# A new decode of the first two weight matrices, and a new order of the first units, in an attention and two-layer MLP kernel

## The chip, the cores and the metric

The kernel runs on one core of one Trainium2 chip. The metric is the device time in microseconds (us). Before the change, three runs took 758.19, 758.59 and 758.95 us, with a median of 758.59 us.

## The reference

Every array arrives on the chip in its stored type. The attention inputs are 32-bit floats. The four weight matrices are 64-bit floats, and the chip has to make 32-bit values of them itself. This is called decoding below. The reference, cut to what matters:

```
state = 0                                          # per batch (4) and head (8): 48 x 48
for t in range(768):                               # gated linear attention
    y[t] = r[t] @ (state + (u * k[t]) outer v[t])
    state = w[t][:, None] * state + k[t] outer v[t]
x = y as (3072 tokens, 384)
h = x @ w_in                                       # 384 -> 1024
solu = h * softmax(h)
ln = (solu - mean) / sqrt(var + 1e-6) * g_ln
x = ln @ w_out                                     # 1024 -> 384
out = max(0.01 * h2, h2) @ w2_out, h2 = x @ w2_in  # 384 -> 2048 -> 384
```

## The kernel before

The 3072 tokens are cut into 24 units of 128 tokens. Six time blocks times four batches give unit i. A unit is prepared by VectorE scans and multiplies (`prep1` to `prep4`, `prep_k`, `prep_diag`), runs its attention on TensorE (`att_kt`, `att_scores`, `att_u`, `att_y`), is evacuated by VectorE (`att_x`), turned by TensorE (`x_t`), split into a high and a low part (`x_hi`, `x_lo`) and multiplied with the first weights (`mm1 i half`, nine matmuls of 512 columns for each half). The soft steps and `z_t`, `z_hi`, `z_lo` follow. `mm2a` and `mm2b` multiply three units together with the second weights (12 matmuls of 384 columns each). After all units, `mm3` and `mm4` run the second MLP for groups of 512 tokens.

Every product is made of three passes, high by high, high by low and low by high, so each weight is kept as a high tile (`w1ih`, `w1oh`) and a low tile (`w1il`, `w1ol`).

The schedule is written out by hand. `FIRST` is the text for units 0 to 9, `LOOP` for units 10 to 13 and `LAST` for the rest. Each name in it emits its instructions in that place, so the text sets the order on every engine's queue and on the DMA queue that SyncE issues. An engine runs its own queue in order.

The first weights are decoded inside `FIRST`, in 14 slices. Six slices are of `w_in`, 512 columns each, and eight of `w_out`, 384 columns each. Each slice is a tile `q` of pairs of 32-bit words (lower, upper) that a DMA has brought. Before the change a slice takes these steps.

- `w1_a` (L762): VectorE shifts the exponent out of the upper words (L199), and ScalarE turns it into a power of two (L201, with a bias read per partition).
- `w1_e` (L205, VectorE): the sign is put in.
- `w1_f` (L210, VectorE): the upper 20 mantissa bits are masked out in place.
- `w1_h` (L216, VectorE): the lower words, as floats times 2^-32, are added to them.
- `w1_b` (L221, VectorE): the sum is multiplied with the power of two, and for `w_out` also with `gl` (the factor g_ln).
- `w1_c`: ScalarE rounds the value to the high tile (L803). TensorE puts the value (L805, identity, recorded as two instructions) and minus the high tile (L806) together in the PSUM tile `PO`.
- `w1_d`: ScalarE copies `PO` to the low tile (L812).

`general` (L246) is a slow path for inputs out of range. It stands behind a branch at the end that the given inputs do not take. `mm1 4 0` is called the mark below. It is the first half of unit 4's product with the first weights, the first `mm1` behind all 14 slices.

Of the kernel before, what the change touches and what calls it, by code (L numbers as in the profile page):

```python
# [43 lines left out]
prep_state 1; w1_b; x_t 0; prep1 2; att_scores 1; att_mul_next 1; load_tr 3; x_hi 0; x_lm 0; w1_f; prep_k 2;  # L44
prep_diag 1; x_lo 0; att_evac_s 1; w1_d; prep_check 2; mm1 0 0; w1_c; w1_a; att_state 1; load_o 1; prep2 2; prep3 2;
prep_vd 1; att_kt 2; load_nat 2; w1_d; prep_state 2; w1_a; mm1 0 1; att_evac_k 2; prep1 3; prep_check 3; att_y 1;
att_u 2; prep4 2; soft_max 0; att_x 1; w1_e; load_tr 4; prep_k 3; soft_e 0; x_t 1; att_mid 2; att_scores 2; soft_z
0; w1_f; att_evac_s 2; w1_g; w1_h; prep_bonus 2; x_hi 1; x_lm 1; x_lo 1; mm1 1 0; w1_h; soft_nm 0; prep_check 4; mm1
1 1; soft_c 0; w1_e; w1_b; att_mul_next 2; z_t 0; prep2 3; w1_a; w1_f; w1_c; z_hi 0 0; att_kt 3; prep3 3; z_hi 0 1;
w1_a; w1_d; w1_e; w1_b; w1_h; z_lm 0 0; z_lm 0 1; w1_f; w1_c; w1_b; prep_state 3; z_lo 0 0; prep1 4; z_lo 0 1;  # L50
prep_state 4; prep4 3; w1_d; prep_diag 2; att_scores 3; att_y 2; w1_e; soft_max 1; prep_vd 2; soft_q 0; prep_k 4;
att_x 2; att_state 2; att_evac_k 3; w1_c; x_t 2; load_nat 3; soft_e 1; load_tr 5; x_hi 2; att_u 3; w1_d; att_mid 3;
x_lm 2; x_lo 2; soft_z 1; mm1 2 0; prep_bonus 3; att_evac_s 3; prep2 4; att_kt 4; soft_nm 1; w1_a; w1_f; w1_h;
soft_c 1; w1_e; w1_b; w1_h; w1_c; z_t 1; att_mul_next 3; load_nat 4; w1_a; w1_f; prep3 4; w1_d; mm1 2 1; soft_q 1;
z_hi 1 0; w1_h; w1_b; prep1 5; prep4 4; z_lm 1 0; att_state 3; prep_k 5; prep_diag 3; z_hi 1 1; w1_c; z_lm 1 1;
att_evac_k 4; prep_vd 3; z_lo 1 0; soft_max 2; att_u 4; att_mid 4; att_mul_next 4; z_lo 1 1; att_y 3; w1_d;
att_scores 4; w1_b; att_x 3; soft_e 2; w1_c; x_t 3; att_kt 5; soft_z 2; x_hi 3; prep_bonus 4; att_state 4; w1_e;
# [5 lines left out]
5; prep_k 6; z_t 3; z_hi 3 0; load_tr 7; att_kt 6; att_evac_s 5; z_lm 3 0; z_hi 3 1; mm1 4 1; mm2_out 4; z_lm 3 1;
prep1 7; prep_bonus 6; prep_k 7; mm2a 5; att_scores 6; soft_max 4; prep_state 6; prep_check 6; z_lo 3 0; z_lo 3 1;
prep_vd 5; load_nat 7; prep2 7; prep3 7; att_state 5; att_evac_k 6; load_tr 8; att_y 5; soft_q 3; att_u 6; prep_diag
6; soft_e 4; prep_bonus 7; att_x 5; soft_z 4; prep4 7; att_mid 6; soft_nm 4; att_kt 7; x_t 5; mm2b 5; prep_vd 6;
att_mul_next 6; prep_check 7; x_hi 5; x_lo 5; mm1 5 0; att_evac_s 6; prep1 8; soft_c 4; soft_q 4; z_t 4; load_nat 8;
prep_diag 7; mm1 5 1; z_hi 4 0; prep_vd 7; prep_k 8; z_hi 4 1; att_evac_k 7; z_lo 4 0; prep2 8; att_state 6; z_lo 4
1; load_tr 9; att_y 6; att_u 7; mm2_out 5; soft_max 5; att_x 6; prep_state 7; att_scores 7; att_kt 8; soft_e 5; x_t
6; prep_bonus 8; mm2a 6; att_mid 7; prep3 8; soft_z 5; att_mul_next 7; soft_nm 5; x_hi 6; mm2b 6; prep_state 8;  # L70
att_evac_k 8; x_lo 6; load_nat 9; mm1 6 0; prep_check 8; prep1 9; prep2 9; soft_c 5; soft_q 5; z_t 5; z_hi 5 0;
prep4 8; prep_bonus 9; att_evac_s 7; z_hi 5 1; z_lo 5 0; load_tr 10; mm1 6 1; mm2_out 6; att_state 7; z_lo 5 1;
prep_k 9; soft_max 6; att_u 8; att_y 7; att_scores 8; prep3 9; soft_e 6; att_x 7; mm2a 7; prep4 9; prep_check 9;
prep_diag 8; prep_diag 9; x_t 7; soft_z 6; load_nat 10; att_mid 8; mm2b 7; x_hi 7; x_lo 7; soft_nm 6; soft_c 6; mm1
7 0; att_mul_next 8; att_evac_s 8; z_t 6; prep_vd 8; z_hi 6 0; prep_state 9; att_kt 9; load_tr 11; att_state 8;
prep1 10; z_lo 6 0; z_hi 6 1; prep_k 10; z_lo 6 1; mm1 7 1; soft_max 7; att_y 8; prep_state 10; att_scores 9; soft_q
6; mm2_out 7; att_evac_k 9; prep2 10; att_x 8; prep_vd 9; att_u 9; soft_e 7; att_mid 9; att_kt 10; x_t 8; x_hi 8;
att_mul_next 9; mm2a 8; soft_z 7; att_evac_k 10; att_state 9; x_lo 8; soft_nm 7; soft_c 7; prep3 10; prep_check 10;
prep1 11; att_evac_s 9; mm1 8 0; z_t 7; mm1 8 1; z_hi 7 0; z_lo 7 0; z_hi 7 1; z_lo 7 1; soft_q 7; prep_bonus 10;
att_y 9; att_u 10; prep2 11; prep_check 11; prep_k 11; prep4 10; att_scores 10; prep3 11; prep_state 11; soft_max 8;  # L80
att_x 9; load_nat 11; mm2b 8; load_tr 12; prep_diag 10; x_t 9; soft_e 8; soft_z 8; att_mid 10; mm2_out 8; att_evac_s
10; att_kt 11; att_mul_next 10; soft_nm 8; mm2a 9; x_hi 9; prep4 11; x_lo 9; prep1 12; soft_c 8; soft_q 8; mm1 9 0;
# [1029 lines left out]
```

## Time and profile before

| what | value |
|---|---|
| median of three runs | 758.59 us |
| the profiled execution | 758.94 us |
| its span, first to last instruction | 757.2 us |
| around the span | 1.74 us |
| TensorE busy | 725.6 us (96%) |
| VectorE busy | 505.7 us (67%) |
| ScalarE busy | 359.9 us (48%) |

The spans of the engines overlap. In the rows, PE is TensorE's matmul, PEld its weight load, DVE VectorE, ACT ScalarE, POOL GpSimd and SPq the DMA queue. The time around the span is not seen by the profile. The rows of consecutive matmuls overlap (a row of 0.39 us, and the next one starts 0.23 us after it), so their spacing is read from their starts or from a run of many.

### The profile page before, as it was taken

What the parts mean: (1) busy time and instruction counts of PE and PEld (TensorE: products, weight loads), DVE (VectorE), ACT (ScalarE), POOL (GpSimd) and SP (SyncE); (2) the same over time, 40 slices, a digit from 0 to 9 for tenths busy, and PEclk for the clock granted to TensorE, in tenths of its full rate; (3) what the DMA queues carried; (4) which work ended last, traced back from release to release, by engine and by line L of the source; (5) the groups of instructions that cost most, each with busy time, mean ns of one, the idle gap of its engine ahead of it and who ended that gap; (6) DMA issues with size and microseconds to landing.
All of it is one profiled execution on the core that took longest, in us unless ns stands there. A gap on an engine that the chain in (4) does not pass through costs nothing.

```text
span 757.2 us, 15011 instructions
## 1 busy us (share of the span) xinstructions
PE 725.6 (96%) x6209; PEld 612.1 (81%) x6209; DVE 505.7 (67%) x851; ACT 359.9 (48%) x660; POOL 164.2 (22%) x184
## 2 busy tenths in 40 slices
PE   2799999999999999998999999999999999999996
PEld 1466889898989898997888888888888888888885
DVE  7799979878878888877899975453343334334332
ACT  4487675656565554665645543323232332332231
POOL 2335554455553434312000100001000100100000
PEclk9999999999999999999999999999999999999999
DMA  9723263344354343224363220050020001001001
GB/s 333 272 76 132 91 186 120 108 132 159 99 171 138 120 146 116 65 84 140 102 218 106 84 62 1 1 166 1 1 84 1 1 0 42 1 0 42 1 0 45
DMA packets 30606, 69.07 MB, mean 91 GB/s; under 512 B 3244, under 2 KB 15684, under 8 KB 30404
## 3 DMA queue, kind: packets, MB, share of 16 engines
q1 hardware_dynamic: 30532, 68.06, 27.0%
q8 instruction: 50, 0.82, 0.4%
q14 instruction: 24, 0.20, 0.1%
HBM read 58.59 MB, written 9.45 MB: 90 GB/s over the span
## 4 chain that ended last, share of the span: by engine, by line
PE 88%; DVE 8%; ACT 2%; issue 1%; DMA 1%; POOL 0%; SPq 0%; DVEq 0%
PE PK L915 13%; PE PZ L915 13%; PE PH L665 11%; PE PO L721 10%; PE PH L944 9%; PE PA L944 9%; PE PO L944 4%; PE PZ L944 4%; PE PZ L632 3%; PE PZ L613 3%; PE PA L721 2%; PE PZ L622 1%; PE PA L550 1%; PE PO L805 1%; PE PA L570 1%
## 5 line engine op out<-in xcount | busy, mean ns | idle before, releaser
L935 DVE TENSOR_TENSOR gw<-t,gh 128x512 fp32r<-128x512 f32 x96 | 68.4, 714 | 52.5 <-ACT gh L931 52.3
L931 ACT CAST gh<-t 128x512 fp32r<-128x512 f32 x96 | 59.6, 621 | 67.0 <-DVE t L927 51.5
L927 DVE TENSOR_TENSOR t<-t,PZ 128x512 f32<-128x512 f32 x48 | 32.9, 686 | 69.3 <-ACT t L923 69.2
L901 POOL TENSOR_TENSOR x2l<-x2l,x2h 128x1536 fp32r<-128x1536 f32 x4 | 14.1, 3531 | 287.5 <-ACT x2h L897 287.5
L927 DVE TENSOR_TENSOR t<-t,PK 128x512 f32<-128x512 f32 x48 | 33.0, 687 | 59.4 <-ACT t L923 59.2
L923 ACT ACTIVATE t<-PZ 128x512 f32<-128x512 f32 x48 | 28.7, 598 | 84.1 <-PE PZ L915 79.3
L923 ACT ACTIVATE t<-PK 128x512 f32<-128x512 f32 x48 | 28.7, 598 | 80.4 <-PE PK L915 75.0
L721 PE MATMUL PO<-zh,w1oh 128*128 128x384 f32 x168 | 59.8, 356 | 0.0
L665 PE MATMUL PH<-w1ih,xh 128*128 128x512 f32 x144 | 58.0, 403 | 0.8 <-DVE zbuf L677 0.8
L665 PE MATMUL PH<-w1ih,xl 128*128 128x512 f32 x144 | 56.8, 395 | 0.2
L665 PE MATMUL PH<-w1il,xh 128*128 128x512 f32 x144 | 56.5, 392 | 0.0
L721 PE MATMUL PO<-zh,w1ol 128*128 128x384 f32 x168 | 56.3, 335 | 0.0
L721 PE MATMUL PO<-zl,w1oh 128*128 128x384 f32 x168 | 56.3, 335 | 0.0
L915 PE MATMUL PK<-x2h,w2ih 128*128 128x512 f32 x144 | 56.2, 390 | 0.0
L915 PE MATMUL PK<-x2l,w2ih 128*128 128x512 f32 x144 | 56.1, 389 | 0.0
L915 PE MATMUL PZ<-x2h,w2il 128*128 128x512 f32 x144 | 56.1, 389 | 0.0
L915 PE MATMUL PZ<-x2l,w2ih 128*128 128x512 f32 x144 | 56.1, 389 | 0.0
L915 PE MATMUL PK<-x2h,w2il 128*128 128x512 f32 x144 | 56.0, 389 | 0.0
L915 PE MATMUL PZ<-x2h,w2ih 128*128 128x512 f32 x144 | 56.0, 389 | 0.0
L673 ACT ACTIVATE ebuf<-PH,nmax 128x1024 f32<-128x1024 f32 x24 | 26.8, 1116 | 39.3 <-DVE nmax L670 39.3
L670 DVE TENSOR_REDUCE nmax<-PH 128x1 f32<-128x1024 f32 x24 | 29.2, 1218 | 15.6 <-PE PH L665 15.5
L944 PE MATMUL PH<-gw,w2oh 128*128 128x512 f32 x96 | 37.4, 389 | 0.0
(189 smaller groups left out, 1955.6 us busy)
## 6 DMA issues: line engine op xcount, KB each, us to landing
tr<-in_trw_dram SPq DMA_DIRECT2D x23, 776.0 KB, 5.0
natq<-in_nat_q_dram SPq DMA_DIRECT2D x24, 384.0 KB, 4.6
w2s<-in_moe_w_in_dram SPq DMA_DIRECT2D x48, 128.0 KB, 2.6
w2s<-in_moe_w_out_dram SPq DMA_DIRECT2D x16, 384.0 KB, 3.2
natv<-in_nat_v_dram SPq DMA_DIRECT2D x24, 192.0 KB, 4.4
o_dram<-o SPq DMA_DIRECT2D x24, 192.0 KB, 1.9
x2l<-o_dram SPq DMA_DIRECT2D x6, 768.0 KB, 6.0
out_dram<-ot SPq DMA_DIRECT2D x18, 256.0 KB, 2.1
```

What stands on the lines that cost most here:

```text
L613: pe.matmul(out=y[64 * c:64 * c + 64, hs], lhsT=s[64 * c:64 * c + 64, x, q], rhs=a[64 * c:64 * c + 64, h], start=(h == 0), stop=False, ski ...
L632: pe.matmul(out=out, lhsT=x, rhs=ident, is_transpose=True, start=(n == 0), stop=(n == of - 1), skip_group_check=True)
L665: pe.matmul(out=PH[:, half], lhsT=a[:, kc], rhs=c[:, kc, 512 * half:512 * half + 512], start=(n == 0), stop=(n == 8))
L670: dve.tensor_reduce(out=nmax[:, i:i + 1], in_=flat(PH), axis=AX.X, op=ALU.max, negate=True)
L673: act.activation(out=ebuf, in_=flat(PH), func=AF.Exp, bias=nmax[:, i:i + 1], accum_out=s_all[:, i:i + 1])
L721: pe.matmul(out=o2[m], lhsT=a[:, c, 128 * m:128 * m + 128], rhs=d[:, c], start=(c == 0 and q == 0), stop=(c == K1 - 1 and q == 2))
L915: pe.matmul(out=h_at[n % 2], lhsT=a[:, kc, 128 * o:128 * o + 128], rhs=d[:, kc], start=(q == 0), stop=(q == 8))
L923: act.activation(out=gs[n][0], in_=h_at[n % 2], func=AF.Copy, scale=0.01)
L927: dve.tensor_tensor(out=t, in0=t, in1=h_at[n % 2], op=ALU.max)
L931: act.copy(out=gh, in_=t)
L935: dve.tensor_tensor(out=gw, in0=t, in1=f(gh), op=ALU.subtract)
L944: pe.matmul(out=at, lhsT=a[:, c % 4, 128 * o:128 * o + 128], rhs=d, start=(c == 0 and q == 0), stop=(c == K2 - 1 and q == 2))
```

## The change

The decode of the 14 slices is made of other steps, the sizes staying as they are. ScalarE reads the upper words as 32-bit floats and multiplies them by 2^-112 (`w1_a`). VectorE shifts the bits left by three (`w1_e`) and puts the sign in (`w1_f`), which gives the value without the lower words, in `t`. VectorE masks `t` to its signed power of two (`w1_h`), and multiplies that with the lower words and -2^-52 (for `w_out` also with g_ln) into the low tile itself (`w1_b`). In `w1_c` ScalarE multiplies a slice of `w_out` by g_ln, then rounds to the high tile, and TensorE adds a third product, minus the low tile, between the two others. `w1_d` is unchanged and overwrites the low tile.

The names in `FIRST` are the same 546 items in another order. `general` is rewritten with inner loops in place of unrolled code and with its decoded weights in DRAM. An unused pad of 96 columns becomes `gl2`, which holds g_ln times -2^-52. `LOOP` and `LAST` are unchanged.

```diff
 FIRST = """
-w1_a; prep1 0; load_w 1; prep_state 0; w1_e; prep2 0; load_w 2; load_w 3; load_tr 1; w1_f; prep3 0; prep_k 0; w1_h;
-load_nat 0; att_kt 0; prep_check 0; prep4 0; w1_a; w1_a; w1_b; w1_e; w1_e; w1_f; w1_c; w1_d; att_evac_k 0; load_o 0;
-w1_f; w1_h; w1_h; w1_a; w1_a; w1_b; w1_e; w1_c; w1_b; w1_e; att_u 0; load_g; load_u; w1_a; prep1 1; w1_f; load_nat
-1; w1_e; prep2 1; w1_h; prep_k 1; prep_check 1; prep3 1; w1_a; prep_bonus 0; w1_d; w1_f; att_scores 0; w1_b; att_kt
-1; prep4 1; w1_h; w1_f; w1_c; att_evac_k 1; att_mid 0; att_mul_next 0; prep_diag 0; w1_h; prep_vd 0; att_evac_s 0;
-att_state 0; w1_d; w1_b; w1_c; att_y 0; att_u 1; prep_bonus 1; load_tr 2; w1_d; att_mid 1; att_x 0; w1_e; w1_c;
...
-4; att_scores 5; prep_state 5; prep2 6; soft_q 2; att_mid 5; prep_bonus 5; soft_e 3; prep_check 5; mm2a 4; soft_z 3;
-soft_nm 3; x_t 4; x_hi 4; mm2b 4; att_mul_next 5; soft_c 3; prep3 6; load_nat 6; x_lo 4; mm1 4 0; prep4 6; prep_diag
...
+load_w 1; w1_a; prep1 0; w1_a; load_w 2; w1_e; w1_a; prep_k 0; w1_f; att_kt 0; prep2 0; w1_h; prep3 0; att_evac_k 0;
+load_w 3; w1_b; prep4 0; w1_e; w1_c; w1_a; load_tr 1; w1_e; w1_f; w1_f; w1_h; prep_check 0; w1_e; w1_d; w1_h; w1_f;
+w1_b; load_nat 0; w1_b; w1_a; w1_h; w1_c; w1_e; w1_b; w1_a; w1_d; w1_f; prep1 1; w1_c; w1_e; att_u 0; w1_h; prep_k
+1; load_u; w1_d; att_scores 0; load_tr 2; prep2 1; w1_c; prep_bonus 0; w1_d; att_kt 1; att_evac_k 1; w1_f; att_mid
+0; prep3 1; att_mul_next 0; prep_diag 0; prep_vd 0; prep_check 1; w1_b; att_evac_s 0; prep_check 2; load_nat 1;
+prep_state 0; att_y 0; att_state 0; w1_h; att_x 0; att_u 1; prep4 1; load_o 0; att_mid 1; prep1 2; w1_c; x_t 0;
+prep_state 1; w1_b; load_g; prep_bonus 1; w1_d; load_nat 2; load_tr 3; prep2 2; x_hi 0; att_mul_next 1; att_scores
+1; prep_diag 1; w1_c; w1_a; att_state 1; x_lm 0; x_lo 0; mm1 0 0; prep_k 2; att_evac_s 1; att_kt 2; w1_a; prep_vd 1;
...
+4; soft_e 3; prep_k 6; att_u 5; prep_check 5; load_nat 6; att_scores 5; prep2 6; att_kt 6; att_x 4; prep_bonus 5;
+soft_z 3; prep_state 6; x_t 4; att_mid 5; x_hi 4; x_lo 4; soft_nm 3; soft_c 3; att_evac_s 5; prep3 6; prep_check 6;
+load_tr 7; att_mul_next 5; prep_bonus 6; mm2a 4; mm1 4 0; prep_diag 5; z_t 3; mm1 4 1; z_hi 3 0; att_evac_k 6; z_lm
+3 0; prep4 6; z_hi 3 1; z_lm 3 1; prep1 7; mm2b 4; load_tr 8; att_scores 6; prep_vd 5; prep2 7; soft_max 4; soft_q
...
-        const.tile([128, 96], F32, name="pad")
+        gl2 = const.tile([128, 96], F32, name="gl2")[:, 0:K1]
...
-            decode_exp(nc, q, t, ebias)
+            act.activation(out=f(t), in_=f(q[:, :, 1]), func=AF.Copy, scale=2.0 ** -112)
...
+            top = q[:, :, 1]
             if n == 0:
-                decode_sign(nc, q, t)
+                dve.tensor_scalar(out=t, in0=t, scalar1=3, scalar2=None, op0=ALU.logical_shift_left)
             elif n == 1:
-                decode_top(nc, q)
+                dve.scalar_tensor_tensor(out=t, in0=top, scalar=-2147483648, in1=t, op0=ALU.bitwise_and,
+                                         op1=ALU.bitwise_or)
             elif n == 2:
-                decode_sum(nc, q)
+                dve.tensor_scalar(out=top, in0=t, scalar1=-8388608, scalar2=None, op0=ALU.bitwise_and)
             else:
-                x = f(q[:, :, 0])
-                decode_mul(nc, q, t, x, 2.0 ** -20 if key[0] == "i" else gl[:, key[1]:key[1] + 1])
-                w1_done.append((key, x))
+                dve.scalar_tensor_tensor(
+                    out=w1_home(key)[1], in0=q[:, :, 0].bitcast(U32),
+                    scalar=-2.0 ** -52 if key[0] == "i" else gl2[:, key[1]:key[1] + 1], in1=f(top),
+                    op0=ALU.mult, op1=ALU.mult)
+                w1_done.append((key, f(t)))
                 return
...
+            hi, lo = w1_home(key)
+            if key[0] == "o":
+                act.activation(out=t, in_=t, func=AF.Copy, scale=gl[:, key[1]:key[1] + 1])
             act.copy(out=hi, in_=t)
             d = PO[:, 0:t.shape[1]]
             pe.matmul(out=d, lhsT=ident, rhs=t, start=True, stop=False)
+            pe.matmul(out=d, lhsT=minus, rhs=lo, start=False, stop=False)
             pe.matmul(out=d, lhsT=minus, rhs=hi, start=False, stop=True)
...
-                pool.tensor_scalar(out=gl, in0=gl, scalar1=2.0 ** -20, scalar2=None, op0=ALU.mult)
+                pool.tensor_scalar(out=gl2, in0=gl, scalar1=-2.0 ** -52, scalar2=None, op0=ALU.mult)
```

## Rows read from the trace of the kernel before

**Rows 1.** The page: busy time of each engine over the span, share, instructions.
```profile
span 757.2 us, 15011 instructions
PE 725.6 (96%) x6209; PEld 612.1 (81%) x6209; DVE 505.7 (67%) x851; ACT 359.9 (48%) x660; POOL 164.2 (22%) x184
```

**Rows 2.** Table by stretch: length, busy time by engine, clock, DMA share, GB/s.
```profile
5.07:38.00 32.93, 19.84 (x205) 11.37 (x206) 28.01 (x48) 14.55 (x29) 8.05 (x7) 1.00 0.85 323
38.00:91.50 53.50, 49.91 (x658) 38.62 (x658) 51.35 (x93) 42.71 (x86) 24.20 (x28) 1.00 0.28 95
91.50:169.80 78.30, 77.84 (x1138) 70.11 (x1137) 64.25 (x99) 47.68 (x94) 41.00 (x48) 1.00 0.43 139
```

**Rows 3.** Timeline, TensorE: first matmul of `mm1` of units 0, 4 and 23.
```profile
38.00 0.39 PE L665 MATMUL PH<-w1ih,xh 128*128 128x512 f32 x1
91.49 0.39 PE L665 MATMUL PH<-w1ih,xh 128*128 128x512 f32 x1
332.42 0.39 PE L665 MATMUL PH<-w1ih,xh 128*128 128x512 f32 x1
```

**Rows 4.** Groups by line, VectorE, 5 to 100 us: count, busy us, mean ns.
```profile
L559 DVE COPY_PREDICATED ss<-mask,PA 128x512 f32<-128x512 int32 x6 | 4.4, 731 | 0.3 <-ACT ao L584 0.3
L216 DVE SCALAR_TENSOR_TENSOR zl<-zl 128x384 f32<-128x384 uint32 x4 | 2.2, 553 | 0.1
L216 DVE SCALAR_TENSOR_TENSOR zh<-zh 128x384 f32<-128x384 uint32 x4 | 2.1, 550 | 0.0
L216 DVE SCALAR_TENSOR_TENSOR zl<-zl 128x512 f32<-128x512 uint32 x3 | 2.0, 667 | 0.0
L216 DVE SCALAR_TENSOR_TENSOR zh<-zh 128x512 f32<-128x512 uint32 x3 | 2.0, 687 | 0.0
L210 DVE TENSOR_SCALAR zl<-zl 128x384 int32<-128x384 int32 x4 | 1.4, 360 | 0.0
L210 DVE TENSOR_SCALAR zl<-zl 128x512 int32<-128x512 int32 x3 | 1.2, 410 | 0.0
```

**Rows 5.** Timeline, the first decode steps and `prep1 0`.
```profile
5.07 0.43 DVE L199 TENSOR_SCALAR ebuf<-zh 128x512 int32<-128x512 int32 x1 [2.89 <-DMA zh<-in_w1p_dram]
5.53 0.72 ACT L201 ACTIVATE ebuf<-ebuf,ebias 128x512 int32<-128x512 int32 x1 [3.04 <-DVE ebuf L199]
5.82 1.24 DVE L482 TENSOR_TENSOR_SCAN suf<-tr,sel 112x520 f32<-112x520 f32 x1 [0.32 <-DMA tr<-in_trw_dram]
```

**Rows 6.** Groups by line, ScalarE, 5 to 100 us.
```profile
L201 ACT ACTIVATE w2s<-w2s,ebias 128x384 int32<-128x384 int32 x8 | 5.0, 619 | 5.2 <-DVE w2s L199 5.2
L803 ACT CAST w1oh<-zh 128x384 fp32r<-128x384 f32 x4 | 2.2, 560 | 0.1
L803 ACT CAST w1ih<-zh 128x512 fp32r<-128x512 f32 x3 | 2.0, 653 | 0.0
L812 ACT CAST w1il<-PO 128x512 fp32r<-128x512 f32 x6 | 3.5, 584 | 5.1 <-PE PO L806 5.0
```

**Rows 7.** Chain of waits in order of time: consecutive matmuls on TensorE.
```profile
103.76 2.09 PE PO L721 x12
105.85 2.09 PE PH L665 x9
113.38 0.53 PE PK L543 x4
```

**Rows 8.** Timeline: two slices' products in `PO`, an early and a later one.
```profile
29.53 2.07 PE L805 MATMUL PO<-zl,ident 128*128 128x512 f32 x2 [0.68 <-ACT w1il L812]
30.61 1.42 PE L806 MATMUL PO<-w1ih,minus 128*128 128x512 f32 x1
35.30 1.17 PE L805 MATMUL PO<-zl,ident 128*128 128x512 f32 x2
```

**Rows 9.** Timeline, VectorE: its longest wait behind the first load.
```profile
34.67 0.56 DVE L628 TENSOR_TENSOR x<-PZ,vd 128x384 f32<-128x384 f32 x1 [4.49 <-PE PZ L622]
```

**Rows 10.** DMA issues: size, us to landing.
```profile
zh<-in_moe_w_out_dram SPq DMA_DIRECT2D x1, 1536.0 KB, 15.7
```

More of the change, by code (lines that the diff above doesn't have):

```diff
@@ L43 @@
-att_state 0; w1_d; w1_b; w1_c; att_y 0; att_u 1; prep_bonus 1; load_tr 2; w1_d; att_mid 1; att_x 0; w1_e; w1_c;
[L44 to L57, printed above, removed]
@@ L63 @@
[L63 to L77, printed above, removed]
@@ L78 @@
[L78 to L82, printed above, removed]
@@ new lines @@
+prep3 2; w1_d; mm1 0 1; att_evac_k 2; load_nat 3; att_y 1; w1_e; prep4 2; prep_state 2; w1_a; prep1 3; w1_f;
+prep_check 3; att_u 2; w1_a; soft_max 0; prep_k 3; att_kt 3; soft_e 0; att_x 1; w1_h; soft_z 0; w1_g; w1_b;
+prep_bonus 2; x_t 1; att_mid 2; prep2 3; att_scores 2; load_tr 4; prep_diag 2; x_hi 1; w1_e; att_evac_s 2; soft_nm
+0; w1_f; x_lm 1; w1_c; x_lo 1; att_mul_next 2; mm1 1 0; w1_e; w1_e; soft_c 0; prep3 3; prep_check 4; prep_state 3;
+w1_f; w1_d; soft_q 0; z_t 0; mm1 1 1; z_hi 0 0; prep4 3; prep_vd 2; w1_h; w1_h; z_lm 0 0; w1_b; prep1 4; z_hi 0 1;
@@ new lines @@
+z_lm 0 1; w1_c; prep_k 4; load_o 1; z_lo 0 0; att_scores 3; w1_b; soft_max 1; z_lo 0 1; w1_f; w1_d; att_y 2; att_x
+2; w1_c; att_evac_k 3; prep_state 4; soft_e 1; att_kt 4; w1_a; att_state 2; soft_z 1; w1_h; x_t 2; prep2 4; x_hi 2;
+w1_e; prep_bonus 3; soft_nm 1; w1_a; att_u 3; prep3 4; x_lm 2; w1_b; x_lo 2; mm1 2 0; soft_c 1; load_tr 5; z_t 1;
+w1_d; w1_e; w1_c; z_hi 1 0; w1_f; att_mid 3; prep4 4; z_lm 1 0; z_hi 1 1; z_lm 1 1; w1_h; att_evac_k 4; att_mul_next
+3; mm1 2 1; w1_a; prep_diag 3; w1_d; load_nat 4; w1_f; z_lo 1 0; att_state 3; prep_vd 3; att_evac_s 3; prep1 5;
@@ new lines @@
+w1_b; prep_k 5; z_lo 1 1; soft_max 2; att_u 4; prep_state 5; w1_h; load_tr 6; att_y 3; soft_q 1; att_mid 4; att_x 3;
+w1_c; soft_e 2; prep_bonus 4; load_nat 5; w1_b; att_scores 4; prep2 5; w1_d; x_t 3; att_mul_next 4; soft_z 2; w1_c;
+att_state 4; w1_e; w1_f; w1_h; x_hi 3; w1_a; soft_nm 2; x_lm 3; w1_e; x_lo 3; w1_f; w1_b; att_kt 5; w1_d; mm1 3 0;
+w1_h; w1_b; soft_c 2; z_t 2; w1_c; z_hi 2 0; mm1 3 1; prep_diag 4; soft_q 2; z_lm 2 0; z_hi 2 1; w1_d; z_lm 2 1;
+w1_c; prep3 5; att_evac_s 4; z_lo 2 0; prep_vd 4; z_lo 2 1; prep1 6; w1_d; soft_max 3; prep4 5; att_evac_k 5; att_y
@@ new lines @@
+prep_check 7; att_mid 6; prep_diag 6; mm2a 5; x_t 5; x_hi 5; x_lo 5; mm2b 5; soft_c 4; att_evac_s 6; mm1 5 0; z_t 4;
+prep_vd 6; att_mul_next 6; prep_state 7; prep3 7; prep1 8; prep4 7; prep2 8; z_hi 4 0; load_nat 7; mm2_out 5; z_hi 4
+1; z_lo 4 0; z_lo 4 1; att_state 6; att_kt 7; soft_q 4; att_evac_k 7; mm1 5 1; load_tr 9; att_y 6; soft_max 5; att_x
+6; att_u 7; prep_bonus 7; att_scores 7; soft_e 5; prep3 8; soft_z 5; prep_diag 7; prep_k 8; load_nat 8; soft_nm 5;
+mm2a 6; x_t 6; x_hi 6; att_mid 7; load_nat 9; x_lo 6; mm2b 6; soft_c 5; mm1 6 0; z_t 5; att_kt 8; prep4 8;
@@ new lines @@
+att_mul_next 7; prep1 9; prep_bonus 8; att_state 7; att_evac_s 7; z_hi 5 0; att_evac_k 8; soft_q 5; z_hi 5 1;
+prep_state 8; mm2_out 6; z_lo 5 0; z_lo 5 1; mm1 6 1; att_u 8; att_scores 8; soft_max 6; att_y 7; prep_check 8;
+soft_e 6; att_mid 8; mm2a 7; prep_vd 7; prep_bonus 9; att_x 7; x_t 7; prep2 9; x_hi 7; prep3 9; prep_k 9; prep_check
+9; load_tr 10; prep4 9; soft_z 6; x_lo 7; soft_nm 6; soft_c 6; prep_diag 8; load_nat 10; mm2b 7; att_mul_next 8;
+load_tr 11; prep_state 9; mm1 7 0; att_evac_s 8; z_t 6; mm2_out 7; z_hi 6 0; att_state 8; z_hi 6 1; att_kt 9;
@@ new lines @@
+att_evac_k 9; prep_vd 8; prep1 10; prep_k 10; prep_diag 9; prep_vd 9; z_lo 6 0; mm1 7 1; prep_check 10; z_lo 6 1;
+prep_bonus 10; soft_max 7; att_y 8; att_scores 9; load_nat 11; att_u 9; soft_q 6; att_x 8; att_kt 10; att_evac_s 9;
+x_t 8; soft_e 7; mm2a 8; soft_z 7; soft_nm 7; x_hi 8; x_lo 8; prep_check 11; mm1 8 0; att_evac_k 10; att_mid 9;
+att_mul_next 9; prep_diag 10; soft_c 7; z_t 7; prep2 10; z_hi 7 0; mm1 8 1; mm2b 8; prep_bonus 11; z_hi 7 1; prep1
+11; prep3 10; z_lo 7 0; att_state 9; att_u 10; z_lo 7 1; prep_diag 11; prep4 10; soft_max 8; prep_vd 10; prep_k 11;
@@ L86 @@
+att_y 9; prep_state 10; att_x 9; mm2_out 8; soft_q 7; att_scores 10; prep2 11; prep3 11; mm2a 9; att_mid 10; prep4
+11; att_mul_next 10; load_tr 12; x_t 9; soft_e 8; mm2b 9; x_hi 9; soft_z 8; soft_nm 8; x_lo 9; prep_vd 11; mm1 9 0;
+soft_c 8; z_t 8; prep_state 11; att_evac_s 10; load_nat 12; att_kt 11; z_hi 8 0; load_tr 13; z_hi 8 1; att_evac_k
+11; prep1 12; mm1 9 1; prep2 12; z_lo 8 0; soft_q 8; prep_bonus 12; mm2_out 9; prep_check 12; z_lo 8 1; att_state
+10; prep_k 12
 """
@@ L396, in body @@
+        for o in range(KC):
+            sp.dma_start(
+                out=out[128 * o:128 * o + 128].rearrange("p (i t) -> p i t", t=128),
+                in_=y_dram[:, :, o].rearrange("i p t -> p i t"),
+            )
 def body(tc, trw, nat_q, nat_v, w1p, u_p, g_p, r, k, v, w, u, w1i, w1o, gln, w2i, w2o, out):
```

276 lines of the change are left out of this document (134 added, 142 removed).

## The prediction, made before the changed kernel ran

> **What bounds the kernel now.** I read the page first: TensorE is busy 96% of the span [rows 1], so a saving elsewhere counts only where TensorE is kept waiting. The table by stretch says where that is. From 5.07 us, when the first weights land, to 91.5 us, VectorE is busy 79.4 of 86.4 us (28.01 + 51.35) and ScalarE 57.3 [rows 2]. The reader is to see that a busy TensorE there is no dense one: 658 matmuls in the 53.5 us from 38 on, against 1138 in the 78.3 us behind. The timeline shows the same by progress. Unit 0's `mm1` starts at 38.00 and unit 4's, the mark, at 91.49, so 13.4 us for a unit, though these units have no `mm2` yet. From unit 4 to unit 23 a unit takes (332.42 - 91.49) / 19 = 12.68 us with its `mm2`, of 24 matmuls at 2.09 / 12 = 0.174 us, 4.2 us in all [rows 3, 7]. Without it TensorE could do a unit in some 8.5 us, and with the slices' own products (below) in about 10. So up to the mark VectorE sets the pace, and behind it TensorE does. The granted clock is listed as 1.00, the 2.4 GHz level, in every stretch; still, a slice's first product took 2.07 us at 29.53 and 1.17 us at 35.30 [rows 2, 8].
>
> So the sum is made at the mark. All 14 slices lie ahead of it in both orders. What VectorE has to do ahead of it gives its time, and what TensorE has left behind it gives the end.
>
> **The change, part by part.** *VectorE, decode.* Five instructions a slice become four. The shift by three stands for L199, the sign is L205 again, the mask is one like L210, and the last multiply is L221 with an integer operand as L216 has; I price each like the row it replaces. What goes is the sum, L216: 2.2 + 2.1 + 2.0 + 2.0 = 8.3 us for 14 [rows 4]. The unseen forms are the shift and the mask. The shift has one operation and not two, and the mask reads `t` and writes every second word. At worst a mask costs what the two-tensor form L216 does, 0.28 us more than L210 at 512 columns and 0.19 at 384 [rows 4], so 6 x 0.28 + 8 x 0.19 = 3.2 us more. At best each of the 28 is a quarter of L210's 0.36 us cheaper, an estimate, 2.5 us less. I take neither, since L210 is the nearest row to both.
>
> *VectorE, start.* Today L199 runs at 5.07, before `prep1 0` can start at 5.82 for its own DMA [rows 5]. Now VectorE's first step waits for ScalarE's (0.72 us from 5.07), so this slot is lost and the 0.43 us come later. +0.43.
>
> *VectorE, order.* Counting the names ahead of the mark in both texts, the only VectorE item more is `att_evac_s 5`, 0.73 us [rows 4]. +0.7. Sum at the mark: -8.3 + 0.4 + 0.7 = -7.2 us, so the mark moves from 91.5 to about 84.3.
>
> *TensorE, behind the mark.* `mm2b 4` stood ahead of the mark and now stands behind it: 12 matmuls, 2.09 us. `att_kt 6` has gone ahead of it: 4 matmuls, 0.53 us [rows 7]. +1.6 us.
>
> *TensorE, ahead of the mark.* Each slice has one matmul more, at 0.232 us for 512 columns (2.09 / 9) and 0.174 for 384 [rows 7]: 6 x 0.232 + 8 x 0.174 = 2.8 us. Early matmuls take twice that [rows 8], so 4.2 at most. I cost it at nothing: minus the low tile needs nothing of ScalarE and runs while ScalarE writes the high tile, and the work that hides it is VectorE's, with about 10 us for a unit on TensorE against 12 to 13. If that cover is gone it costs its 2.8 to 4.2 us.
>
> *ScalarE.* The first step keeps its place with a constant factor and no bias tile. Its nearest row is the cast L803, 0.65 and 0.56 us against 0.72 and 0.62 now [rows 5, 6], so 0 to -0.9 us over 14. By the Trainium skill ("ScalarE: Activation LUTs", "What ACT_TABLE_LOAD costs") an activation with constant scale and bias takes 186 ns and 0.833 ns an element, 0.61 and 0.51 us here, which as an estimate would be 1.5 us less over the 14; its figure with a bias tile, 0.71 us, agrees with the row's 0.72 [rows 5]. The factor g_ln adds eight instructions of 0.56 to 0.62 us, 4.5 to 5.0 us. `prep_check 6`, two steps over 512 columns of about 0.7 us like L201's and the reading of their sums, is ahead of the mark now, another 1.7 as an estimate. ScalarE's 57.3 us become 61 to 64, of 79 us up to the new mark: 80%, from 66%. I cost this at nothing on the path, hidden by VectorE's 72 us; its price when not hidden is the second rival.
>
> *Waits and queues.* The hop from VectorE to ScalarE at the head of each slice goes; ScalarE sat idle 5.2 us for it in the later slices [rows 6]. The slice's `t` is now held until its `w1_c`. In the text each `w1_a` that takes one of the four buffers again stands behind the `w1_c` of the slice that had it, so nothing new waits there. On the DMA queue `load_u` moves ahead of `load_o 0`, which took 15.7 us to land [rows 10], and `load_o 0` goes behind `load_tr 2`, which waits for unit 0's last reader. Up to `load_o 0` some 8.3 MB (by the shapes in the loads' calls) must pass at the 323 GB/s of that stretch [rows 2], so it lands at about 27 us, an estimate. ScalarE's `w1_a` for the seventh slice needs it and stands ahead of `x_lo 0` in the text, near 30 us. The cover is some 3 us; a later landing would hold ScalarE, and `mm1 0 0` with it, by as much.
>
> *The rest.* `general` is not run, and `gl2` takes the pad's place. Code that isn't run lies outside the 757.2 us, and what it could touch is the 1.74 us around the span at most; I take nothing.
>
> **The sum.** -7.2 + 1.6 = -5.6 us. From the profiled execution, 757.2 + 1.74 - 5.6 = 753.3. That execution, 758.94, stands 0.35 us above the median of the runs, so for the median I predict 753.0 us.
>
> **The rivals.** *More: the stall goes too.* VectorE's largest wait, 4.49 us at 30.2, is `att_x 0` behind TensorE's `att_y 0` [rows 9], which stood on TensorE's queue behind four early slices' products of 3.1 us each (from 29.53 to 32.03 on TensorE, and 0.58 for the copy) [rows 6, 8]. In the new text `att_y 0` is ahead of the fifth slice and the fourth slice comes sooner. If the whole wait goes, 753.0 - 4.5 = 748.5. Against it: each of those products is longer by one matmul, some 0.46 us at half speed, and VectorE, with less to do, comes to `att_x 0` sooner. My forecast keeps the wait as it is.
>
> *Slower: TensorE's queue stands behind ScalarE.* For the eight slices of `w_out`, the identity product now waits for ScalarE's multiply by g_ln, issued only at `w1_c`, behind whatever ScalarE has in hand; before, it waited for VectorE alone. TensorE runs in order, so everything behind it waits. With 0.6 us for the multiply and one other step ahead of it (0.72 us like L201 [rows 5]), a slice costs 1.3 us, eight cost 10.6, and the mark comes 3.4 us later than today: 753.0 + 10.6 = 763.6. From 5.6 / 8 = 0.70 us a slice on, nothing is won. For it: ScalarE goes to 80%. Against it: that is one in five idle, and the text can put `w1_c` late enough. In a sentence of its own: the Trainium skill's "ScalarE: Activation LUTs" ("Rules for kernel authors") says to do plain multiplies on VectorE and not on ScalarE, and so stands on this rival's side; the rows alone leave that open, since VectorE is the fuller engine here.
>
> *The same: the decode sets no pace.* If what is won at the mark is lost up to 169.8 us, where ScalarE, GpSimd and VectorE serve TensorE in a new order (77.84 of 78.3 us busy [rows 2], but units not evenly apart), the time stays at 757.1 to 760.1.
>
> **How the numbers follow.** My forecast, a gain of 2 to 8 us (its own range 750.5 to 756.6), gets 0.55; the larger gain 0.17; the same 0.11; slower 0.17. What a measurement of this kernel can tell is about 0.2%, 1.5 us. Faster is 0.72, the same 0.11, slower 0.17. For eight in ten the range goes from 748.0, where the stall is gone too, to 760.0; beyond lie most of the slower case and the largest gains. The unseen forms' -2.5 to +3.2 us lie within it.
>
> **What would show it.** The mark, the first `mm1` of unit 4, at 84 us (82 to 88), and unit 0's at 32 to 35. Fourteen `L216` fewer on VectorE and its other decode rows at 0.34 to 0.69 us. Behind the mark, the same spacing of units, 12.7 us. ScalarE near 80% busy up to the mark, and TensorE's identity products of 384 columns not waiting for it by more than 0.7 us each. The prediction is wrong if the mark stands later than 88 us, if the strided mask costs like a two-operand form, or if the units behind the mark come further apart.

## The result, and the profile of the changed kernel

The changed kernel takes 750.36 us (median of 4 runs, 749.37 to 751.64) against 758.77 for the kernel before beside it (758.19 to 760.28): the ratio is 0.9887, its 95% interval 0.9866 to 0.9908. It is 8.4 us faster; 5.6 were forecast. The profiled execution took 751.64 us, the longest of the four, so the two profiles lie 7.3 us apart and not 8.4.

The page of the changed kernel, in the form of [rows 1]:

```profile
span 749.9 us, 15039 instructions
PE 725.5 (97%) x6223; PEld 614.0 (82%) x6223; DVE 499.4 (67%) x837; ACT 362.0 (48%) x668; POOL 168.6 (22%) x184
```

Its table by stretch (length; busy time and count of TensorE, its weight loads, VectorE, ScalarE and GpSimd; granted clock, DMA share, GB/s), as [rows 2], up to unit 0's first `mm1`, up to the mark, and behind it:

```profile
5.07:34.70 29.63, 20.52 (x215) 12.38 (x216) 26.07 (x45) 16.45 (x35) 13.14 (x9) 0.83 0.85 313
34.70:82.80 48.10, 47.49 (x655) 37.91 (x654) 43.73 (x82) 43.46 (x89) 23.89 (x28) 1.00 0.39 133
82.80:162.60 79.80, 79.52 (x1146) 71.74 (x1144) 67.37 (x99) 47.12 (x94) 40.77 (x46) 1.00 0.40 137
```

Its timeline at the first matmul of `mm1` of units 0, 4 and 23, as [rows 3]:

```profile
34.66 0.40 PE L670 MATMUL PH<-w1ih,xh 128*128 128x512 f32 x1
82.75 0.39 PE L670 MATMUL PH<-w1ih,xh 128*128 128x512 f32 x1
325.41 0.39 PE L670 MATMUL PH<-w1ih,xh 128*128 128x512 f32 x1
```

The whole gain lies ahead of the mark, which moved from 91.49 to 82.75 us, 8.7 us. Behind it the kernel takes 1.4 us more (749.9 - 82.8 = 667.1, against 757.2 - 91.5 = 665.7). Up to the mark VectorE was busy 28.01 + 51.35 = 79.4 us and idle 7.1 [rows 2]; now it is busy 26.07 + 43.73 = 69.8 and idle 7.9. Its busy time went down by 9.6 us, somewhat more than the mark moved. But look at the second line: between unit 0 and the mark TensorE is now busy 47.49 of 48.10 us, where it was 49.91 of 53.50. There VectorE is no longer the engine with the least room.

The decode's groups on VectorE, 5 to 100 us (count, busy us, mean ns), to be set beside [rows 4]:

```profile
L787 DVE TENSOR_SCALAR w2s<-w2s 128x384 int32<-128x384 int32 x8 | 2.7, 343 | 0.0
L792 DVE TENSOR_SCALAR zl<-w2s 128x384 int32<-128x384 int32 x4 | 1.4, 356 | 0.0
L794 DVE SCALAR_TENSOR_TENSOR w1ol<-zl,gl 128x384 fp32r<-128x384 uint32 x4 | 2.4, 607 | 0.0
...
L792 DVE TENSOR_SCALAR zl<-w2s 128x512 int32<-128x512 int32 x2 | 0.8, 416 | 0.0
L787 DVE TENSOR_SCALAR w2s<-w2s 128x512 int32<-128x512 int32 x2 | 0.8, 410 | 0.0
```

The shift (L787) and the strided mask (L792) cost what L210 did, 0.36 and 0.41 us. ScalarE's, to be set beside [rows 6]:

```profile
L815 ACT ACTIVATE w2s<-w2s,gl 128x384 f32<-128x384 f32 x8 | 5.0, 629 | 0.0
L776 ACT ACTIVATE w2s<-zl 128x384 f32<-128x384 f32 x4 | 2.3, 567 | 0.0
L776 ACT ACTIVATE ebuf<-zh 128x512 f32<-128x512 f32 x2 | 1.3, 664 | 6.9 <-DMA zh<-in_w1p_dram 6.9
```

The last line holds more than its length: it is ScalarE that now stands 6.9 us for the first two loads, 2.7 and 4.2. In the kernel before, VectorE stood 2.89 us for the first of them [rows 5].

### The profile page after: what moved, and what is told of

It reads as the page before. It is cut to its first block, busy times and chain, and to the rows that moved or that the text cites. A ratio compares the mean times of both kernels' runs of the same rounds, so it can differ in the third digit from the quotient of the medians.

```text
span 749.9 us, 15039 instructions
## 1 busy us (share of the span) xinstructions
PE 725.5 (97%) x6223; PEld 614.0 (82%) x6223; DVE 499.4 (67%) x837; ACT 362.0 (48%) x668; POOL 168.6 (22%) x184
## 4 chain that ended last, share of the span: by engine, by line
PE 91%; DVE 5%; issue 1%; ACT 1%; DMA 1%; POOL 0%; SPq 0%; DVEq 0%
PE PK L929 13%; PE PZ L929 13%; PE PH L670 12%; PE PO L726 11%; PE PA L958 9%; PE PH L958 9%; PE PO L958 4%; PE PZ L958 4%; PE PZ L637 4%; PE PZ L618 3%; PE PA L726 2%; PE PZ L627 2%; PE PA L555 1%; PE PA L575 1%; PE PO L818 1%
## 5 line engine op out<-in xcount | busy, mean ns | idle before, releaser
L915 POOL TENSOR_TENSOR x2l<-x2l,x2h 128x1536 fp32r<-128x1536 f32 x4 | 14.1, 3535 | 287.4 <-ACT x2h L911 287.4
L958 PE MATMUL PH<-gh,w2ol 128*128 128x512 f32 x96 | 37.4, 389 | 0.0
```

The costliest lines, as they stand in the source:

```text
L958: pe.matmul(out=at, lhsT=a[:, c % 4, 128 * o:128 * o + 128], rhs=d, start=(c == 0 and q == 0), stop=(c == K2 - 1 and q == 2))
```

## The experiments

All times are medians, and each ratio is against the kernel before run beside it. An interval is some 0.2% to either side, so two runs 2 us apart are hardly told apart by time.

**The change taken apart.** `order_only` has the old decode with the new text of `FIRST`, `decode_only` the new decode with the old text. `sums_back` puts a step in the form of the old sum back into each slice. `no_third` leaves out the product of the low tile, and so its part of the weights.

```
sums_back, in w1_h, the third of a slice's four steps (ahead of the mask)
...
+                dve.scalar_tensor_tensor(out=w1_home(key)[0], in0=q[:, :, 0].bitcast(U32), scalar=2.0 ** -32, in1=top,
+                                         op0=ALU.mult, op1=ALU.add)
...
no_third, in w1_c
-    pe.matmul(out=d, lhsT=minus, rhs=lo, start=False, stop=False)
```

> The new decode in the old order of the first units. If VectorE's 14 sums are what counts, most of the gain is here: 752 to 755 us, and VectorE's wait for unit 0's attention stays near 4.5 us. If the new order is what counts, the time stays within 1.5 us of before, 757 to 760. If the two only work together (the old order places the products in PO and the ScalarE steps for the old decode), the time is at or above before, 758 to 763.

> The old decode in the new order of the first units. If VectorE's sums are what counts, the 8.3 us of sums are back and the gain is gone: 757 to 762 us. If the new order is what counts, by the shorter wait for unit 0's attention and the earlier loads, the time stays at 750 to 754.

> The changed kernel with one more VectorE instruction in each of the 14 slices, of the form of the old sum; its result goes to the high tile, which ScalarE overwrites afterwards, so the output is the same. If VectorE sets the pace up to unit 4, the mark comes 8.3 us later and the time is 757 to 760 us. If VectorE has slack in the new order, it stays under 754.

> The changed kernel without the added third product on TensorE; the lower words are left out of the value. If TensorE's 14 more matmuls are hidden up to the mark, as forecast, the time is that of the changed kernel, 749 to 751.5 us. If they are on the path, it is 2.8 to 4 us less, 746 to 748.

Measured: `decode_only` 756.19 us (0.9962, 0.9948 to 0.9977), `order_only` 767.26 (1.0121, 1.0105 to 1.0136), `sums_back` 757.04 (0.9981, 0.9973 to 0.9990), `no_third` 747.70 (0.9859, 0.9845 to 0.9873); the kernel before took 758.39 beside them. So the decode alone gives 2.2 us, the order alone costs 8.9, and both together give 8.4: neither edit has a price of its own. Tables by stretch of `decode_only`, then `order_only`, split at unit 0's `mm1` and ended at the mark:

```profile
5.07:35.40 30.33, 20.45 (x211) 12.21 (x212) 23.43 (x41) 14.00 (x29) 9.11 (x7) 0.83 0.92 352
35.40:89.30 53.90, 51.15 (x666) 40.29 (x665) 46.69 (x86) 46.19 (x94) 24.02 (x28) 1.00 0.29 98
```

```profile
5.07:42.00 36.93, 19.14 (x209) 10.16 (x210) 31.17 (x51) 17.36 (x35) 13.35 (x9) 0.97 0.68 252
42.00:97.70 55.70, 50.73 (x647) 39.27 (x646) 48.61 (x90) 40.05 (x82) 23.69 (x28) 0.92 0.34 116
```

In `decode_only` VectorE's work is as light as in the changed kernel, 70.1 us, and yet the mark moved only 2.2: VectorE is idle 14.1 us in place of 7.1. Less work on it turned into waiting. Its waits, and one of ScalarE's (engine, what waited <- for what: us in total, times, longest):

```profile
DVE x L633 <- PE PZ L627: 6.3, 4, 4.3
...
ACT w2s L776 <- DMA zh<-in_moe_w_out_dram: 3.3, 1, 3.3
```

The stall of [rows 9] stands there nearly whole, 4.3 us, and ScalarE waits 3.3 for `load_o 0`. In the changed kernel the stall's longest is 2.2 us and there is no wait for that load. So the lighter VectorE gains its time only in the new order. Which of the order's moved items does it isn't shown. In `order_only` VectorE's first wait is of another kind:

```profile
DVE ebuf L199 <- DMA zh<-in_w1p_dram: 5.9, 2, 3.0
```

`sums_back` against the changed kernel gives the sums' price in the new order: 6.7 us, of the 8.3 in the sum. Its table, split and ended in the same way:

```profile
5.07:37.20 32.13, 21.10 (x215) 11.80 (x216) 30.66 (x51) 16.45 (x35) 9.66 (x9) 0.95 0.76 285
37.20:88.70 51.50, 48.71 (x654) 37.67 (x653) 48.70 (x90) 43.90 (x88) 25.04 (x28) 1.00 0.36 127
```

Yet `order_only` and `sums_back` have almost the same VectorE work up to the mark (79.8 and 79.4 us) and lie 10.2 us apart. VectorE's total can't be the whole of it.

**The head of a slice.** `hop` gives VectorE the first step of a slice again and takes the shift from it, so that its count of instructions stays. `decode_only_hop` is the same in the old order, `hop_late` the same for the last ten slices only.

```
-    act.activation(out=f(t), in_=f(q[:, :, 1]), func=AF.Copy, scale=2.0 ** -112)
+    dve.tensor_scalar(out=t, in0=q[:, :, 1], scalar1=-1, scalar2=None, op0=ALU.bitwise_and)
+    act.activation(out=f(t), in_=f(t), func=AF.Copy, scale=2.0 ** -112)
...
-                dve.tensor_scalar(out=t, in0=t, scalar1=3, scalar2=None, op0=ALU.logical_shift_left)
+                pass
```

> The changed kernel, with the first step of a slice on VectorE again: VectorE copies the upper words to the slice's tile, ScalarE scales that tile in place, and the shift by three is left out for it (so the first weights come out too small). VectorE has as many instructions as in the changed kernel and nearly the same busy time, since a strided copy takes 0.43 and 0.36 us and the shift took 0.41 and 0.34; only the place differs: VectorE's copy stands at the head of the slice, where the load comes in, and ScalarE waits for VectorE. Theory 1, VectorE's total up to the mark sets the pace: the mark at 82.8 to 83.5 us and 750 to 751 us in all. Theory 2, the step at the head matters with this order, because VectorE then waits in order for the loads: the old decode in the new order was 10.2 us slower than the changed kernel with a sum put back, so the mark at 87 to 92 us and 755 to 760 us in all, with VectorE's waits on the loads of the first slices back.

> The new decode in the old order (756.2 us), with VectorE's copy at the head of a slice in place of its shift by three (left out, so that the first weights come out too small). In the new order the same edit cost 8.9 us. Theory 1, a step of VectorE at the head costs because ScalarE has to wait for it in any order: 763 to 767 us. Theory 2, it costs because the new order asks for slices and loads at places that only suit a head on ScalarE: in the old order 755 to 758 us.

> The changed kernel, with VectorE's copy at the head (and the shift by three left out) for the last ten of the 14 slices alone; the first four keep ScalarE's step at the head. With the copy at the head of all 14, the time was 8.9 us more, unit 0's first mm1 2.8 us later and the mark 7.2 us later: VectorE stood 3.0 us at the second slice's copy for its load, and unit 0's keys came 3.3 us later behind it. Theory 1, both parts are real: the wait for the first loads costs 3 us, which goes, and the rest comes from the later slices, so 755.5 to 757 us and the mark at 86 to 88 us. Theory 2, all of it follows from the late start: 750 to 751.5 us. Theory 3, the late start is made good and the later slices set it: 758 to 760 us.

Measured: `hop` 759.27 us (1.0012, 1.0000 to 1.0025), `decode_only_hop` 757.84 (0.9993, 0.9984 to 1.0002), `hop_late` 757.31 (0.9984, 0.9973 to 0.9994). The same edit costs 8.9 us in the new order and 1.65 in the old (2.4 by the ratios, give or take 1.3). So theory 2 of `decode_only_hop` held: the price of a head on VectorE is that of the new order, which is written for a head on ScalarE. What happens at the start shows in VectorE's timeline, in the changed kernel and then in `hop`:

```profile
5.94 1.24 DVE L487 TENSOR_TENSOR_SCAN suf<-tr,sel 112x520 f32<-112x520 f32 x1 [3.76 <-DMA tr<-in_trw_dram]
7.09 0.40 DVE L787 TENSOR_SCALAR ebuf<-ebuf 128x512 int32<-128x512 int32 x1
7.56 0.69 DVE L498 TENSOR_TENSOR kt<-tr,suf 112x512 f32<-112x512 f32 x1
```

```profile
6.01 1.24 DVE L487 TENSOR_TENSOR_SCAN suf<-tr,sel 112x520 f32<-112x520 f32 x1 [0.28 <-DMA tr<-in_trw_dram]
10.21 0.43 DVE L776 TENSOR_SCALAR ebuf<-zh 128x512 int32<-128x512 int32 x1 [2.95 <-DMA zh<-in_w1p_dram]
10.55 0.42 DVE L776 TENSOR_SCALAR zbuf<-zh 128x512 int32<-128x512 int32 x1
10.89 0.68 DVE L498 TENSOR_TENSOR kt<-tr,suf 112x512 f32<-112x512 f32 x1
```

The new text asks for the second slice right behind `prep1 0`. With VectorE at the head, that slice's load, not yet landed, holds `kt` from 7.56 to 10.89 us, and unit 0's `mm1` comes at 37.5 us. In the changed kernel it comes at 34.7, and in `no_scale`, `diag` and `scale_twice` (below), which have the same work up to 43 us, at 31.9, 33.4 and 33.8: one execution tells that time to 3 us and no better. `hop_late` takes this part away and gains 2.0 us on `hop`, where 3 were expected; the 6.9 us that it is slower than the changed kernel come later, as its first theory has it, though its time and its mark, 88.1, are both just past the 757 and the 88 given. Tables by stretch of `hop`, then `hop_late`:

```profile
5.07:37.50 32.43, 19.82 (x215) 10.76 (x215) 26.17 (x43) 15.92 (x34) 9.97 (x8) 1.00 0.72 268
37.50:90.00 52.50, 47.97 (x654) 37.84 (x654) 47.66 (x84) 43.70 (x90) 24.62 (x30) 1.00 0.38 133
```

```profile
5.07:35.40 30.33, 20.81 (x215) 11.38 (x216) 26.21 (x43) 15.87 (x34) 7.51 (x8) 0.83 0.78 289
35.40:88.10 52.70, 48.02 (x655) 37.86 (x654) 47.76 (x84) 43.79 (x90) 24.83 (x30) 1.00 0.38 133
```

Between unit 0 and the mark `hop_late` takes 4.6 us more than the changed kernel. ScalarE stands 9.3 us in eight waits for VectorE's copies. But a second thing is mixed in. Up to the mark VectorE has 127 instructions in the changed kernel, in `hop` and in `hop_late` alike, and is busy 69.8, 73.8 and 74.0 us. So of the 7.2 us by which the mark of `hop` lies later, 4.0 are VectorE steps that took longer, and 3.2 are idle time, 11.1 us in place of 7.9. The longest of these steps ran beside GpSimd (see the last section). No run separates the two causes, so the 8.9 us aren't all shown to be the queue's.

**ScalarE.** `scale_twice` does the multiplication by g_ln twice, `no_scale` not at all. `diag` keeps the computation and gives the multiplication to TensorE and to the step that writes the high tile.

```
diag, in w1_c, for a second weight
-    act.activation(out=t, in_=t, func=AF.Copy, scale=gl[:, key[1]:key[1] + 1])
-    act.copy(out=hi, in_=t)
+    act.activation(out=hi, in_=t, func=AF.Copy, scale=gl[:, key[1]:key[1] + 1])
-    pe.matmul(out=d, lhsT=ident, rhs=t, start=True, stop=False)
+    pe.matmul(out=d, lhsT=gd[key[1]], rhs=t, start=True, stop=False)
diag, beside the slice's mask
+    pool.tensor_scalar(out=gd[k], in0=ident, scalar1=gl[:, k:k + 1], scalar2=None, op0=ALU.mult)
```

> The changed kernel with the multiplication by g_ln on ScalarE done twice (so g_ln comes into the upper part of the second weights squared): eight more instructions of 0.63 us, 5.0 us of ScalarE up to the mark, which takes it from 59.9 to 65 us of 82.8 (78%). Theory 1, ScalarE's work is hidden, as the prediction put it: 750.4 us within 0.7. Theory 2, TensorE's queue stands behind each multiply: 8 times 0.63, 755.4 us, and the mark at 88 us.

> The changed kernel without the multiplication by g_ln on ScalarE (the upper part of the second weights then lacks g_ln). A second multiplication cost 4.6 us. Theory 1, only ScalarE's last few per cent count, and the first multiplication was hidden: 749.7 to 751.1 us. Theory 2, ScalarE sets the pace between unit 0's first mm1 and the mark (21.5 of 22.8 us busy from 60 us on), and the multiplication costs its 5.0 us as it stands: 745.4 to 746.5 us, the mark at 78 to 79 us.

> The changed kernel, with the whole computation kept: ScalarE writes the high tile of a second weight's slice as the value times g_ln in one step, and TensorE's first product takes a diagonal matrix of g_ln in place of the identity; GpSimd makes that matrix, eight steps of 128 columns more on an engine that is busy 24 of 48 us up to the mark. If theory 2 of the run without the multiplication holds, 745.5 to 747 us, as without it. If the multiplication was hidden, 750.4 within 0.7. A rival: GpSimd's step comes late in its queue and TensorE waits for it, 750 to 754 us, with waits of the first product on GpSimd.

Measured: `scale_twice` 754.93 us (0.9954, 0.9933 to 0.9976), `no_scale` 749.54 (0.9898, 0.9882 to 0.9913), `diag` 751.59 (0.9920, 0.9906 to 0.9933). The first multiplication is hidden within what a run can tell (0.8 us), the second costs 4.6 of its 5.0. For `scale_twice` theory 2 named the time, 755.4 us, but not the place: its mark came at 86.7 and not at 88, and TensorE waited for the multiplication only 1.8 us, in three waits. Table by stretch of `scale_twice` from 60 us to its mark:

```profile
60.00:86.70 26.70, 25.33 (x343) 19.99 (x342) 23.44 (x45) 25.67 (x52) 13.64 (x16) 1.00 0.26 86
```

ScalarE is busy 25.67 of 26.70 us, the fullest engine. That speaks for an engine that has run out of room, but part of the 4.6 us may be the clock: in this execution it was down, near 0.50, from about 44.6 to 48.0 us, where the changed kernel's was at 1.00. `no_scale` ended a little under the range of its theory 1 (749.7 to 751.1), and its theory 2 (745.4 to 746.5) fell. `diag`, the one try at a faster kernel here that moved work, gains nothing: there was nothing to gain from ScalarE. Its TensorE showed no wait for GpSimd, so the rival's mechanism fell, though its range of times was met. VectorE was 3.0 us busier there up to the mark, beside a GpSimd with eight more steps; whether that is the 1 us more isn't shown, and 1 us lies near what the intervals allow.

**TensorE's waits and its clock.** `two_tiles` puts every other early slice's products into another PSUM tile, so that they don't wait until ScalarE has emptied the one; `filler` adds nine unread matmuls where TensorE waited 2.4 us for VectorE.

```
two_tiles, in w1_c (w1_n counts the slices)
+    early_d = {1: PH[:, 0], 3: PH[:, 0], 5: PH[:, 1]}
-    d = PO[:, 0:t.shape[1]]
+    d = early_d.get(w1_n[0], PO)[:, 0:t.shape[1]]
filler, called ahead of att_y 0
+    for _ in range(9):
+        pe.matmul(out=PH[:, 1], lhsT=minus, rhs=w1ih[:, 0, 0:512], start=True, stop=True)
```

> The changed kernel, with the second, fourth and sixth slices' products in another PSUM tile, so that a slice's identity product no longer waits until ScalarE has read the low tile of the slice before. Theory 1, the third product costs 2.7 us because it makes this chain of TensorE and ScalarE over the one tile longer: unit 0's first mm1 at 33 to 34 us against 34.7, and 748.4 to 749.4 us in all. Theory 2, the product costs because TensorE's own time ahead of unit 0's mm1 counts: no change, 749.9 to 750.9 us.

> The changed kernel with nine matmuls of 512 columns more, whose results nobody reads, ahead of unit 0's first product with the state, where TensorE waited 2.4 us for VectorE (from 23.4 to 25.8 us) before its granted clock stood at half from 25.3 to 32.1 us. Theory 1, the idle time lets the clock fall and the fall costs: no half clock from 25 to 32 us, unit 0's first mm1 1 to 2 us sooner (33 to 34 us) and 748.5 to 749.5 us in all. Theory 2, the clock's fall is hidden behind VectorE or has another cause: the mark and the time stay within 0.7 us of 750.4. Theory 3, the added matmuls run later than the wait: 2 us more, 752.4.

Measured: `two_tiles` 750.43 us (0.9900, 0.9880 to 0.9920), `filler` 752.19 (0.9927, 0.9902 to 0.9953). Neither gains. `two_tiles` had unit 0's `mm1` at 33.5 us, within what the same early work shows above, and the time stayed, as its theory 2 has it. In `filler` TensorE was busy all through the wait. The stretch from 25 to 30 us, in the changed kernel and in `filler`:

```profile
25.00:30.00 5.00, 4.19 (x81) 3.78 (x82) 2.70 (x7) 2.88 (x8) 3.50 (x4) 0.53 0.41 131
```

```profile
25.00:30.00 5.00, 5.00 (x97) 4.03 (x96) 3.64 (x6) 4.73 (x13) 3.35 (x5) 1.00 0.45 144
```

The granted clock stays at 1.00 (2.4 GHz) where it was at 0.53 (for most of it the 1.2 GHz level). The early signs of theory 1 came: unit 0's `mm1` at 33.6 us and the mark at 81.7, 1.1 us earlier. Its time did not. The median is nearest to theory 3, 752.4, though the added matmuls did run in the wait; why the time is not below the changed kernel's is open. The medians can't decide theory 1, because the fall is no property of the kernel: of the changed kernel's four executions only the profiled one, the longest, lists a mean clock of 0.992, the others 0.998 or 0.999. `no_scale`, which has the same early work and no filler, shows this stretch so:

```profile
25.00:30.00 5.00, 4.17 (x115) 3.33 (x119) 3.80 (x8) 3.67 (x10) 3.68 (x4) 1.00 0.40 136
```

TensorE had waited 2.5 us there too. So the clock's fall differs from one execution to the next, and the run with the added matmuls doesn't show that they prevented it. What the fall costs is seen in these two executions without a filler. Both start the first matmuls of `att_y 0` at the same time; TensorE's line in the changed kernel, then in `no_scale`:

```profile
25.81 1.62 PE L618 MATMUL PZ<-natv,ss 64*64 64x48 f32 x26 [2.44 <-DVE ss L564]
```

```profile
25.83 0.96 PE L618 MATMUL PZ<-natv,ss 64*64 64x48 f32 x26 [2.46 <-DVE ss L564]
```

From there unit 0's `mm1` comes at 34.66 in the one and at 31.86 in the other, 2.8 us apart. That is most of the 3 us to which one execution tells this time.

## Why the prediction was right, point by point

**The sum at the mark held, by its size: -8.7 us against -7.2.** VectorE's decode went from 38.8 to 28.4 us over the 14 slices (its groups added): 8.3 for the sums, as put, and 2.1 from the remaining steps, which I had priced at no difference; with 0.7 the other way for `att_evac_s 5` that is about the 9.6 us by which VectorE is less busy. Its idle time grew by 0.8. How much of the 2.1 is the edit's isn't shown: up to their marks VectorE took 69.7 us for the same steps in `no_scale`, 69.8 in the changed kernel and 72.2 in `scale_twice`. The shift and the mask cost what L210 did, so the bounds of -2.5 and +3.2 were not needed. Of the other decode rows, forecast at 0.34 to 0.69 us, one group lay outside: two of L789 with a mean of 1.03.

**Behind the mark: +1.4 against +1.6.** `mm2b 4` behind the mark less `att_kt 6` ahead of it was the right count. The spacing of the units, (325.41 - 82.75) / 19 = 12.77 us, is 0.09 us above the 12.68 of the kernel before; over the 19 units that is 1.7 us, the work moved behind the mark.

**The step that failed: "The hop from VectorE to ScalarE at the head of each slice goes", costed at nothing.** Putting a VectorE step back at the head costs 8.9 us in the new order, more than the sums, some 4 of them in longer VectorE steps. I had looked at ScalarE's idle time for it, 5.2 us, and not at what stands in VectorE's queue behind a head that waits for a load. I had even booked the lost slot at the start as +0.43; in the new order, with its early second slice, the move is worth 3.3 us of `kt` there.

**The step that held in size but not in kind: the order as one item of 0.73 us.** By `order_only` the new order costs 8.9 us with the old decode, and by `decode_only` the new decode gives 2.2 with the old order. Counting names ahead of the mark priced VectorE's work, not its waits: it was idle 7.1 us before, 12.9 in `order_only`, 14.1 in `decode_only`, 7.9 in the changed kernel. My sum came out because the two edits together left the idle time nearly as it was, which I had assumed and not shown. That part of the agreement is luck.

**The third products, costed at nothing.** Leaving them out saves 2.7 us by the medians (the ratios differ by 0.0028, with an uncertainty of about 0.0025), the price given for lost cover, 2.8 to 4.2. The cover was VectorE's work, and between unit 0 and the mark little of it is left: TensorE has 0.6 us of room in 48.1. But where the 2.7 us arise isn't settled. Unit 0's `mm1` came at 32.2 us in `no_third`, but at 31.9 in `no_scale`, which has the products; and from there to the mark `no_third` took 47.5 us and the changed kernel 48.1.

**ScalarE's multiplications, costed at nothing,** held, and at the edge: 59.9 of 77.7 us, 77%, against 80% forecast, and the next 5 us cost 4.6, with the clock's part in that open.

**The rivals.** *Slower, TensorE behind ScalarE:* the first products waited 0.5 us in all for the multiplication, where 0.70 us a slice was the point from which it decides. In `scale_twice` it was 1.8 us, so this mechanism is seen there, but it accounts for less than half of the 4.6. The Trainium skill ("ScalarE: Activation LUTs", "Rules for kernel authors") would keep plain multiplies off ScalarE; here one multiply a slice cost nothing that could be measured and a second cost 4.6 us. *More, the stall goes too:* half of it did, 4.49 to 2.2 us, and the time lies between the forecast and that rival's 748.5. The comparison is fair as to the clock: the first 26 matmuls of `att_y 0` took 1.63 us in the kernel before, as slow as the 1.62 of the changed kernel, although the kernel before lists 1.00 for that stretch. So a listed 1.00 doesn't prove the full pace, and the prediction was right to doubt it. The kernel before:

```profile
31.96 1.63 PE L613 MATMUL PZ<-natv,ss 64*64 64x48 f32 x26
```

*The same* fell with the spacing of units. `load_o 0` gave no wait, as estimated.

## What to carry to other kernels

Price a reordering and a change of work together: look at which engine stands at a load in the new text, and what is queued behind it. An instruction at the head of a chain that begins with a transfer can cost its engine's queue and not only its duration: the same step cost 8.9 us in one order and 1.65 in the other, and what it holds up shows in the timeline, 3.3 us of `kt` here. When one engine's work is cut by an eighth, ask at once which engine is the fullest after it: here three engines were above 90% busy, so adding to VectorE or ScalarE cost most of its full price (6.7 of 8.3 us and 4.6 of 5.0), while taking work from ScalarE gave nothing that could be measured.
